# Decode attention, one core: products and folds in place, one exponential per tile with a GpSimd mask, two tiles per value accumulator

## The chip, the cores and the metric

One core of one Trainium2 chip. The metric is the device time of one execution in microseconds (us), here of the single core that runs. Engines in the profile: PE is TensorE (PEld its weight loads), DVE is VectorE, ACT is ScalarE, POOL is GpSimd, SP is SyncE, which issues nearly all loads.

## The reference

One decode step of attention plus a gated MLP, both on the same normalised input. There are 4 sequences (B), 32 heads (H), 4096 cached positions (S), head size 128 (Dh), model size 640 (D).

```python
xn = layernorm(x)                                  # x: [4, 1, 640]
q = (xn @ wq) per head                             # wq: [640, 4096]
scores = einsum('bhqd,bhkd->bhqk', q, k_cache) * Dh ** -0.5
p = softmax(scores)
o = einsum('bhqk,bhkd->bhqd', p, v_cache)          # caches: [4, 32, 4096, 128] bf16
A = o @ wo                                         # wo: [4096, 640]
z = gelu(xn @ w_in); z1, z2 = halves; z2 = layernorm(z2)
B = (z1 * (w_sp * z2 + b_sp)) @ w_out
out = x + A + B
```

The two caches are 128 MiB each and every byte of them is used once.

## The kernel before, in words

**Tiles.** The work is cut into NT = 32 tiles. A tile is HT = 4 heads of one sequence: `i = 4 * hg + b`, head group hg of 8, sequence b of 4. A K tile and a V tile are 4 MiB each: 128 partitions by NC = 128 positions by 128 values, bf16. A partition belongs to one head: each head has LN = 32 partitions ("lanes"), and each lane 128 of its 4096 positions.

**Loads.** All big loads go out on SyncE's queue, in the order of the list `loads`: k0, k1, v0, k2, v1, k3 and so on, each V one place behind the next K; with EXTRA_K two K in a row come at two places (k25 and k26, and k30 and k31 at the end). All tiles share a pool of KV_SLOTS = 5 buffers in ring order, so load n waits until the tile of load n - 5 is no longer used. `pump()` (L121 is the load in `load`) issues what the list `used` allows. `wo` is loaded by head group (`load_wo`, L155 and L153), behind the K and V loads on the same queue. The last V tile is loaded in four pieces (V_CUTS).

**Scores** (per tile, all on 128 partitions). `stage_q` spreads the query rows over the lanes with four matmuls (L383) and a copy (L391). `product` (L397, VectorE) multiplies a quarter of the K tile by the query into the tile `prod`; `fold_half` (L409, VectorE) adds the upper 64 values of each position to the lower 64 into the tile `folded`; `sums` (L421, TensorE) adds up the 64 in eight matmuls with the identity, for each half of the tile, leaving eight values a position in PSUM; `row_sums` (L432, VectorE) adds those eight.

**Softmax.** `lane_max` (L441), `turn_max` (L446, a transpose), `head_max` (L451) and `spread_max` (L462) find each head's maximum and spread its scaled negative over the lanes. `exps` copies it (L470) and runs four exponentials (L474), one per head, each on 32 partitions, writing `p_m[b]` with the other heads' places left at zero, and the sums into `acc`.

**Values.** `blocks` (L489) multiplies V by the masked exponentials, 32 matmuls that take four positions at once and use four groups of 32 output partitions; it copies the accumulator `pv_acc` (L497). `gather` (L506) picks the blocks that belong together into `pv` with `sel`. For the last pieces of the last V tile `pairs` (L518) is used. `group_den` (L530, L534) makes the denominators of a head group, `group_norm` (L539) divides and `group_proj` (L548) multiplies by `wo`.

**Order.** The main part runs under a manual schedule: on TensorE, VectorE, ScalarE and SyncE the instructions run in the order written. In iteration i the softmax of tile i - 1 is interleaved with the products of tile i, and `blocks` runs for a tile `turns[i]` that lags by 1, later by 2 and 3.

Of the kernel before, what the change touches and what calls it, by code (L numbers as in the profile page):

```python
# [20 lines left out]
def kernel(  # L21
# [31 lines left out]
    NQ = 4  # L53
    QC = NC // NQ
# [12 lines left out]
    prod = ctx.enter_context(tc.tile_pool(name="prod", bufs=1))  # L67
    fold = ctx.enter_context(tc.tile_pool(name="fold", bufs=2))
# [80 lines left out]
    def load_wo(j):  # L149
# [19 lines left out]
    scale_row = const.tile([1, P], FP32)  # L169
    nc.vector.memset(scale_row[:], scale_qk)  # L170
# [5 lines left out]
    assert GC * HT <= LN and GC * Dh * 4 <= 2048  # L176
    pv_acc = ps_acc.tile([P, GC * Dh], FP32)
    nc.vector.memset(pv_acc[:], 0.0)
    sel = const.tile([P, GC * HT], FP32)
    nc.vector.tensor_reduce(  # L180
        out=sel[:],
        in_=ident_f[:].rearrange("p (g q) -> p q g", g=CG)[:, 0 : GC * HT, :],
        axis=AX.X,
        op=ALU.add,
    )

    NACC = 2
    p_m = [const.tile([P, NC, HT], BF16, name=f"pm{b}") for b in range(Bsz)]
    acc = [const.tile([P, HT, Bsz], FP32, name=f"acc{g}") for g in range(NACC)]
    for t in p_m + acc:  # L190
        nc.gpsimd.memset(t[:], 0.0)
# [185 lines left out]
    folds, sums_ps, maxes = {}, {}, {}  # L377

    def stage_q(i):
        hg, b = divmod(i, Bsz)  # L380
        qb_ps = ps_m.tile([P, Dh], FP32, tag="m", name="qbc_ps")
        for hh in range(HT):
            nc.tensor.matmul(  # L383
                out=qb_ps[hh * LN : (hh + 1) * LN, :],
                lhsT=qT[:, HT * hg + hh, b : b + 1].to_broadcast([P, LN]),
                rhs=ident[:],
                start=True,
                stop=True,
            )
        qbcs[i] = small.tile([P, Dh], BF16, name="qbc", bufs=3)  # L390
        nc.scalar.copy(out=qbcs[i][:], in_=qb_ps[:])  # L391

    prods = {}

    def product(i, q):
        t = prods[i, q] = prod.tile([P, QC, Dh], BF16, name="prod")
        nc.vector.tensor_tensor(  # L397
            out=t[:],
            in0=k_tiles[i][:, q * QC : (q + 1) * QC, :],
            in1=qbcs[i][:, None, :].to_broadcast([P, QC, Dh]),  # L400
            op=ALU.mult,
        )

    def fold_half(i, q):
        t = prods.pop((i, q))
        half, part = divmod(q, 2)
        if part == 0:
            folds[i, half] = fold.tile([P, HC, HD2], BF16, name="folded")
        nc.vector.tensor_tensor(  # L409
            out=folds[i, half][:, part * QC : (part + 1) * QC, :],  # L410
            in0=t[:, :, 0:HD2],
            in1=t[:, :, HD2:Dh],
            op=ALU.add,
        )

    def sums(i, half):
        t = folds.pop((i, half))
        s = sums_ps[i, half] = ps_s.tile([P, HC, RW], FP32, name="s_ps")
        n = HD2 // RW
        for g in range(n):  # L420
            nc.tensor.matmul(  # L421
                out=s[:],
                lhsT=ident[:],
                rhs=t[:, :, g * RW : (g + 1) * RW],
                start=(g == 0),
                stop=(g == n - 1),
            )
# [16 lines left out]
    def turn_max(i):  # L444
        mT = ps_m.tile([1, P], FP32, tag="m", name="mT")
        nc.tensor.transpose(out=mT[:], in_=maxes[i][:], identity=ident_f[:])  # L446
        maxes[i] = mT

    def head_max(i):
        nm = small.tile([1, HT], FP32, name="nm")  # L450
        nc.vector.tensor_reduce(  # L451
            out=nm[:],
            in_=maxes[i][:].rearrange("a (h p) -> a h p", h=HT),
            axis=AX.X,
            op=ALU.max,
            negate=True,
        )
        maxes[i] = nm

    def spread_max(i):  # L460
        nb_ps = ps_m.tile([P, HT], FP32, tag="m", name="nb_ps")
        nc.tensor.matmul(  # L462
            out=nb_ps[:], lhsT=scale_row[:], rhs=maxes[i][:], start=True, stop=True
        )
        maxes[i] = nb_ps

    def exps(i):
        hg, b = divmod(i, Bsz)
        nb = small.tile([P, HT], FP32, name="nb")
        nc.scalar.copy(out=nb[:], in_=maxes.pop(i)[:])  # L470
        s_sb, pm, a = scores.pop(i), p_m[b], acc[hg % NACC]
        for hh in range(HT):
            ps = slice(hh * LN, (hh + 1) * LN)
            nc.scalar.activation(  # L474
                out=pm[ps, :, hh],
                in_=s_sb[ps, :],
                func=ACT.Exp,
                bias=nb[ps, hh : hh + 1],
                scale=scale_qk,
                accum_out=a[ps, hh, b : b + 1],  # L480
            )

    def blocks(i, c0=0, c1=NC):


        v_nat, pm = v_tiles[i], p_m[i % Bsz]
        for c in range(c0, c1, GC):
            g = c // GC % CG
            nc.tensor.matmul(  # L489
                out=pv_acc[g * LN : g * LN + GC * HT, :],  # L490
                lhsT=pm[:, c : c + GC, :].rearrange("p c h -> p (c h)"),
                rhs=v_nat[:, c : c + GC, :].rearrange("p c d -> p (c d)"),
                start=(c < GC * CG),
                stop=(c >= c1 - GC * CG),
            )
        pv_sb = work.tile([P, GC * Dh], FP32, name="pv_sb")
        nc.scalar.copy(out=pv_sb[:], in_=pv_acc[:])  # L497
        blocks_sb[i] = pv_sb

    def gather(i, stop=True):  # L500
        hg, b = divmod(i, Bsz)
        if b == 0:
            pvs[hg] = ps_pv.tile([P, HT, Bsz], FP32, tag="pv", name="pv")
        pv_sb = blocks_sb.pop(i)
        for k in range(GC):
            nc.tensor.matmul(  # L506
                out=pvs[hg][:, :, b],
                lhsT=pv_sb[:, k * Dh : (k + 1) * Dh],
                rhs=sel[:, k * HT : (k + 1) * HT],
                start=(k == 0),  # L510
                stop=stop and k == GC - 1,
            )

    def pairs(i, c0, c1):
        hg, b = divmod(i, Bsz)
        v_nat, pm = v_tiles[i], p_m[b]
        for c in range(c0, c1):
# [3 lines left out]
                rhs=pm[:, c, :],  # L521
# [6 lines left out]
    def group_den(hg):  # L528
        den = ps_m.tile([P, HT, Bsz], FP32, tag="m", name="den")
        nc.tensor.matmul(  # L530
            out=den[:], lhsT=ones_sq[:], rhs=acc[hg % NACC][:], start=True, stop=True
        )
# [40 lines left out]
    with tc.manual_schedule(engines={E.PE, E.DVE, E.Activation, E.SP}):  # L573
# [5 lines left out]
        for i in range(NT):  # L579
            j = turns.get(i)  # L580
            product(i, 0)
            fold_half(i, 0)
            at(i - 1, row_sums, 1)
            at(i - 1, lane_max)
            at(i - 1, turn_max)
            group(turns.get(i - 1, -1), group_proj)
            product(i, 1)
            at(i - 1, head_max)
            at(i - 1, spread_max)
            at(i - 1, exps)  # L590
            fold_half(i, 1)
            sums(i, 0)
            product(i, 2)
            if i + 2 < NT:
                stage_q(i + 2)
            fold_half(i, 2)
# [10 lines left out]
            product(i, 3)  # L607
            fold_half(i, 3)
# [12 lines left out]
        turn_max(NT - 1)  # L621
        head_max(NT - 1)
        spread_max(NT - 1)
# [3 lines left out]
        gather(NT - 2)  # L627
# [44 lines left out]
```

## Time and profile before

| what | value |
|---|---|
| median of 3 runs | 670.0 us (669.78 to 670.29) |
| the profiled execution's own time | 669.68 us |
| its span | 667.9 us |
| PE busy | 347.9 us (52%) |
| DVE busy | 506.7 us (76%) |
| ACT busy | 113.0 us (17%) |
| POOL busy | 2.7 us |
| read from HBM | 282.24 MB, 423 GB/s over the span |

How to read the lines: a group's line has source line, engine, operation, output from inputs, shapes, count, then total busy us and mean ns of one, then the idle us just before them and what ended it. Section 2 of the page cuts the span into 40 slices; each digit is a busy share in tenths. The chain of waits is followed back from the last instruction. Times in a timeline are us from the start of the span.

### The profile page before, as it was taken

The numbers are of one execution on the slowest core, as the hardware profiler recorded it, in microseconds if no ns is written. First come the engines' busy times: TensorE is split into PE (matmuls) and PEld (weight loads), VectorE is DVE, ScalarE is ACT, GpSimd is POOL, SyncE is SP. The second block draws the span as 40 slices with busy tenths as digits, with TensorE's granted clock in tenths as the row PEclk, the third lists the DMA queues.
The fourth block names the chain that finished last, engine by engine and source line by source line (L and its number), as shares of the span: only waits on it lengthen the run. The fifth ranks groups of instructions, "written<-read, shape, count | busy, mean of one in ns | idle before, by whom it ended". The sixth has DMA issues, their size and how long they took to land.

```text
span 667.9 us, 5968 instructions
## 1 busy us (share of the span) xinstructions
PE 347.9 (52%) x2425; PEld 154.7 (23%) x2425; DVE 506.7 (76%) x435; ACT 113.0 (17%) x361; POOL 2.7 (0%) x13
## 2 busy tenths in 40 slices
PE   1627554535557345663346654455564556546575
PEld 0502221212222122221112221122222112222133
DVE  1299897867789677787777698776787899876961
ACT  0202111101111101111101111111111111110122
POOL 1000000000000000000000000000000000000000
PEclk9997766788766678775786866788766667786677
DMA  9999999999999999999999999999999999999996
GB/s 373 418 440 433 419 433 436 420 435 426 429 426 430 433 430 429 424 431 432 434 421 432 423 434 435 428 426 429 424 435 434 421 430 432 429 422 433 432 422 257
DMA packets 14663, 282.63 MB, mean 423 GB/s; under 512 B 1344, under 2 KB 5548, under 8 KB 5932
## 3 DMA queue, kind: packets, MB, share of 16 engines
q1 hardware_dynamic: 14616, 282.25, 99.1%
q8 instruction: 19, 0.31, 0.2%
q14 instruction: 8, 0.07, 0.0%
q10 hardware_dynamic: 20, 0.01, 0.0%
HBM read 282.24 MB, written 0.01 MB: 423 GB/s over the span
## 4 chain that ended last, share of the span: by engine, by line
DMA 68%; DVE 21%; PE 8%; SPq 1%; issue 1%; DVEq 0%
DMA k_nat<-in_A_k_cache_dram 63%; DVE prod L397 13%; PE s_ps L421 7%; DVE folded L409 5%; DMA v_nat<-in_A_v_cache_dram 5%; DVE s_sb L432 2%; PE pv_acc L489 1%; SPq L121 1%; DVE m L441 1%; DVE nm L451 0%; PE out_ps L548 0%; PE qbc_ps L383 0%; SPq L90 0%; SPq L102 0%; PE den L530 0%
## 5 line engine op out<-in xcount | busy, mean ns | idle before, releaser
L397 DVE TENSOR_TENSOR prod<-k_nat,qbc 128x4096 bf16<-128x4096 bf16 x128 | 292.7, 2287 | 91.4 <-DMA k_nat<-in_A_k_cache_dram 89.9
L421 PE MATMUL s_ps<-folded,ident 128*128 128x512 bf16 x512 | 186.9, 531 | 64.7 <-DVE folded L409 64.6
L409 DVE TENSOR_TENSOR folded<-prod 128x2048 bf16<-128x2048 bf16 x128 | 156.1, 1220 | 3.3
L421 PEld LDWEIGHTS <-ident 128*128 128x128 bf16 x512 | 64.9, 128 | 152.4 <-issue 135.3
L446 PE MATMUL mT<-ident_f,m 128*1 128x128 f32 x32 | 11.0, 344 | 154.8 <-DVE m L441 154.8
L474 ACT ACTIVATE pm<-s_sb,nb 32x128 bf16<-32x128 f32 x128 | 73.9, 578 | 2.6
L470 ACT COPY nb<-nb_ps 128x4 f32<-128x4 f32 x32 | 5.2, 162 | 394.9 <-PE nb_ps L462 394.9
L489 PE MATMUL pv_acc<-v_nat,pm 128*16 128x512 bf16 x1008 | 71.7, 434 | 0.2 <-DMA v_nat<-in_A_v_cache_dram 0.2
L432 DVE TENSOR_REDUCE s_sb<-s_ps 128x64 f32<-128x512 f32 x64 | 43.5, 680 | 7.8 <-PE s_ps L421 5.4
L462 PE MATMUL nb_ps<-nm,scale_row 1*128 1x4 f32 x64 | 18.2, 353 | 56.2 <-DVE nm L451 56.2
L506 PE MATMUL pv<-sel,pv_sb 128*128 128x4 f32 x256 | 34.4, 258 | 19.5 <-ACT pv_sb L497 19.5
L446 PEld LDWEIGHTS mT<-ident_f,m 128*1 128x1 f32 x32 | 2.5, 79 | 173.1 <-DVE m L441 141.8
L506 PEld LDWEIGHTS pv<-sel,pv_sb 128*128 128x128 f32 x256 | 31.6, 195 | 32.3 <-ACT pv_sb L497 32.3
L489 PEld LDWEIGHTS <-pm 128*16 128x16 bf16 x1008 | 26.6, 102 | 32.6 <-issue 17.2
L474 ACT ACTIVATION_READ_ACCUMULATOR pm<-s_sb,nb 32x1 f32 x128 | 32.2, 251 | 0.0
L462 PEld LDWEIGHTS nb_ps<-nm,scale_row 1*128 1x128 f32 x64 | 15.5, 299 | 66.7 <-DVE nm L451 59.8
L497 ACT COPY pv_sb<-pv_acc 128x512 f32<-128x512 f32 x32 | 18.7, 585 | 61.4 <-PE pv_acc L489 61.4
L391 ACT CAST qbc<-qbc_ps 128x128 bf16<-128x128 f32 x32 | 8.4, 265 | 80.0 <-PE qbc_ps L383 80.0
L534 DVE RECIPROCAL rden<-den 128x16 f32<-128x16 f32 x8 | 2.1, 258 | 21.9 <-PE den L530 21.9
L238 DVE CAST qT<-q_ps 128x128 bf16<-128x128 f32 x1 | 0.3, 292 | 15.1 <-PE q_ps L230 15.1
L230 PE MATMUL q_ps<-xnT,wq 128*128 128x4 bf16 x160 | 4.6, 167 | 10.5 <-DMA wq<-in_A_wq_dram 10.5
L441 DVE TENSOR_REDUCE m<-s_sb 128x1 f32<-128x128 f32 x32 | 9.2, 287 | 1.1
(76 smaller groups left out, 79.2 us busy)
## 6 DMA issues: line engine op xcount, KB each, us to landing
k_nat<-in_A_k_cache_dram SPq DMA_DIRECT2D x32, 4096.0 KB, 43.3
v_nat<-in_A_v_cache_dram SPq DMA_DIRECT2D x31, 4096.0 KB, 36.6
wo<-in_A_wo_dram SPq DMA_DIRECT2D x7, 640.0 KB, 44.7
wq<-in_A_wq_dram SPq DMA_DIRECT2D x1, 4096.0 KB, 12.7
w_sb<-in_B_w_in_dram SPq DMA_DIRECT2D x1, 2160.0 KB, 19.5
v_nat<-in_A_v_cache_dram SPq DMA_DIRECT2D x1, 2048.0 KB
wq<-in_A_wq_dram SPq DMA_DIRECT2D x1, 1024.0 KB, 14.8
v_nat<-in_A_v_cache_dram SPq DMA_DIRECT2D x1, 1024.0 KB
```

What stands on the lines that cost most here:

```text
L391: nc.scalar.copy(out=qbcs[i][:], in_=qb_ps[:])
L397: nc.vector.tensor_tensor(out=t[:], in0=k_tiles[i][:, q * QC : (q + 1) * QC, :], in1=qbcs[i][:, None, :].to_broadcast([P, QC, Dh]), op=ALU ...
L409: nc.vector.tensor_tensor(out=folds[i, half][:, part * QC : (part + 1) * QC, :], in0=t[:, :, 0:HD2], in1=t[:, :, HD2:Dh], op=ALU.add,)
L421: nc.tensor.matmul(out=s[:], lhsT=ident[:], rhs=t[:, :, g * RW : (g + 1) * RW], start=(g == 0), stop=(g == n - 1),)
L432: nc.vector.tensor_reduce(out=scores[i][:, half * HC : (half + 1) * HC], in_=sums_ps.pop((i, half))[:], axis=AX.X, op=ALU.add,)
L441: nc.vector.tensor_reduce(out=m1[:], in_=scores[i][:], axis=AX.X, op=ALU.max)
L446: nc.tensor.transpose(out=mT[:], in_=maxes[i][:], identity=ident_f[:])
L462: nc.tensor.matmul(out=nb_ps[:], lhsT=scale_row[:], rhs=maxes[i][:], start=True, stop=True)
L474: nc.scalar.activation(out=pm[ps, :, hh], in_=s_sb[ps, :], func=ACT.Exp, bias=nb[ps, hh : hh + 1], scale=scale_qk, accum_out=a[ps, hh, b : ...
L489: nc.tensor.matmul(out=pv_acc[g * LN : g * LN + GC * HT, :], lhsT=pm[:, c : c + GC, :].rearrange("p c h -> p (c h)"), rhs=v_nat[:, c : c + ...
L497: nc.scalar.copy(out=pv_sb[:], in_=pv_acc[:])
L506: nc.tensor.matmul(out=pvs[hg][:, :, b], lhsT=pv_sb[:, k * Dh : (k + 1) * Dh], rhs=sel[:, k * HT : (k + 1) * HT], start=(k == 0), stop=sto ...
```

## The change

- `product` and `fold_half` work on half a K tile instead of a quarter, and write into the K tile itself; the tiles `prod` and `folded` and their pools are gone. `sums` reads its input from the K tile.
- The maximum is found without the transpose: `lay_max` (ScalarE) lays each lane's maximum on a diagonal, one matmul with `head_scale` spreads a head's 32 maxima over its lanes, and `head_max` (VectorE) reduces them on all 128 partitions.
- `exps` is one exponential on 128 partitions into a new tile `p`; a GpSimd multiplication by a head mask spreads it into `p_m[b]`.
- `blocks` of an even and the following odd tile add into one accumulator, whose 32 rows a group now hold both tiles (each tile's `p_m` is zero in the other's half). Copy and `gather` run for odd tiles alone.
- `group_den` multiplies the sums by the mask on GpSimd first.
- `stage_q` transposes the 16 query rows of a head group once in four tiles, and spreads them with one matmul per tile instead of four.
- The main loop's order follows: two products and two folds an iteration. `used`, `pump` and KV_SLOTS are as before.

```diff
-    def product(i, q):
-        t = prods[i, q] = prod.tile([P, QC, Dh], BF16, name="prod")
+    def product(i, half):
+        t = k_tiles[i][:, half * HC : (half + 1) * HC, :]
         nc.vector.tensor_tensor(
-            out=t[:],
-            in0=k_tiles[i][:, q * QC : (q + 1) * QC, :],
-            in1=qbcs[i][:, None, :].to_broadcast([P, QC, Dh]),
+            out=t,
+            in0=t,
+            in1=qbcs[i][:, None, :].to_broadcast([P, HC, Dh]),
             op=ALU.mult,
         )
...
+        t = k_tiles[i][:, half * HC : (half + 1) * HC, :]
         nc.vector.tensor_tensor(
-            out=folds[i, half][:, part * QC : (part + 1) * QC, :],
...
+            out=t[:, :, 0:HD2], in0=t[:, :, 0:HD2], in1=t[:, :, HD2:Dh], op=ALU.add
         )
...
     def sums(i, half):
-        t = folds.pop((i, half))
+        t = k_tiles[i][:, half * HC : (half + 1) * HC, :]
...
+    def lay_max(i):
+
+        d = small.tile([P, LN], FP32, name="lay")
+        nc.scalar.activation(
+            out=d[:], in_=lane_diag[:], func=ACT.Copy, scale=maxes[i][:, 0:1]
+        )
+        maxes[i] = d
+
+    def spread_max(i):
+        ps = ps_m.tile([P, LN], FP32, tag="m", name="max_ps")
+        nc.tensor.matmul(
+            out=ps[:], lhsT=head_scale[:], rhs=maxes[i][:], start=True, stop=True
+        )
+        maxes[i] = ps
...
-        for hh in range(HT):
-            ps = slice(hh * LN, (hh + 1) * LN)
-            nc.scalar.activation(
-                out=pm[ps, :, hh],
-                in_=s_sb[ps, :],
-                func=ACT.Exp,
-                bias=nb[ps, hh : hh + 1],
-                scale=scale_qk,
-                accum_out=a[ps, hh, b : b + 1],
-            )
+        nb = maxes.pop(i)
+        p = small.tile([P, NC], BF16, name="p")
+        nc.scalar.activation(
+            out=p[:],
+            in_=scores.pop(i)[:],
+            func=ACT.Exp,
+            bias=nb[:],
+            scale=scale_qk,
+            accum_out=acc[hg % NACC][:, b : b + 1],
+        )
+        e = b % 2 * GC * HT
+        nc.gpsimd.tensor_tensor(
+            out=p_m[b][:, :, e : e + GC * HT].rearrange("p g (c h) -> p g c h", h=HT),
+            in0=p[:].rearrange("p (g c) -> p g c", c=GC)[:, :, :, None].to_broadcast(
+                [P, NC // GC, GC, HT]
+            ),
+            in1=hmask_bf[:, None, None, :].to_broadcast([P, NC // GC, GC, HT]),
+            op=ALU.mult,
+        )
...
-                out=pv_acc[g * LN : g * LN + GC * HT, :],
-                lhsT=pm[:, c : c + GC, :].rearrange("p c h -> p (c h)"),
+                out=pv_acc[g * LN : (g + 1) * LN, :],
+                lhsT=pm[:, c // GC, :],
                 rhs=v_nat[:, c : c + GC, :].rearrange("p c d -> p (c d)"),
-                start=(c < GC * CG),
-                stop=(c >= c1 - GC * CG),
+                start=(i % 2 == 0 and c < GC * CG),
+                stop=(i % 2 == 1 and c >= c1 - GC * CG),
             )
+        if i % 2 == 0:
+            return
...
     def group_den(hg):
+        own = small.tile([P, HT, Bsz], FP32, name="own_sum")
+        nc.gpsimd.tensor_tensor(
+            out=own[:],
+            in0=acc[hg % NACC][:, None, :].to_broadcast([P, HT, Bsz]),
+            in1=hmask[:, :, None].to_broadcast([P, HT, Bsz]),
+            op=ALU.mult,
+        )
...
             product(i, 0)
-            fold_half(i, 0)
             at(i - 1, row_sums, 1)
             at(i - 1, lane_max)
-            at(i - 1, turn_max)
+            at(i - 1, lay_max)
+            at(i - 1, spread_max)
             group(turns.get(i - 1, -1), group_proj)
+            fold_half(i, 0)
+            at(i - 1, head_max)
+            at(i - 1, exps)
+            sums(i, 0)
             product(i, 1)
-            at(i - 1, head_max)
-            at(i - 1, spread_max)
-            at(i - 1, exps)
-            fold_half(i, 1)
-            sums(i, 0)
-            product(i, 2)
             if i + 2 < NT:
                 stage_q(i + 2)
-            fold_half(i, 2)
...
             row_sums(i, 0)
-            product(i, 3)
-            fold_half(i, 3)
+            fold_half(i, 1)
             if due:
                 gather(due[-1])
             for jj in due:
                 group(jj, group_norm)
             sums(i, 1)
             used.add(("k", i))
             pump()
```

## The prediction

> **What bounds the kernel now.** I read the page from the top: the busy shares, the forty slices, the DMA queue, then the costliest groups.
>
> ```profile
> PE 347.9 (52%) x2425; PEld 154.7 (23%) x2425; DVE 506.7 (76%) x435; ACT 113.0 (17%) x361; POOL 2.7 (0%) x13
> DMA  9999999999999999999999999999999999999996
> GB/s 373 418 440 433 419 433 436 420 435 426 429 426 430 433 430 429 424 431 432 434 421 432 423 434 435 428 426 429 424 435 434 421 430 432 429 422 433 432 422 257
> q1 hardware_dynamic: 14616, 282.25, 99.1%
> ...
> L397 DVE TENSOR_TENSOR prod<-k_nat,qbc 128x4096 bf16<-128x4096 bf16 x128 | 292.7, 2287 | 91.4 <-DMA k_nat<-in_A_k_cache_dram 89.9
> L421 PE MATMUL s_ps<-folded,ident 128*128 128x512 bf16 x512 | 186.9, 531 | 64.7 <-DVE folded L409 64.6
> L409 DVE TENSOR_TENSOR folded<-prod 128x2048 bf16<-128x2048 bf16 x128 | 156.1, 1220 | 3.3
> ```
>
> No engine is full, VectorE least far from it at 76%. The one load queue is: 282.25 MB, packets under way 99.1% of the time, a nine in every slice but the last. VectorE's largest idle time, 89.9 of 91.4 us before its products, is waiting for K to land.
>
> The chain of waits, in order of time, then gives the beat (columns: start, length, what).
>
> ```profile
> 163.09 2.30 DVE prod L397
> ...
> 177.72 0.33 SPq L121
> ...
> 223.24 2.30 DVE prod L397
> ...
> 323.43 2.29 DVE L397 TENSOR_TENSOR prod<-k_nat,qbc 128x4096 bf16<-128x4096 bf16 x1 [3.70 <-DMA k_nat<-in_A_k_cache_dram]
> ...
> 343.01 2.29 DVE L397 TENSOR_TENSOR prod<-k_nat,qbc 128x4096 bf16<-128x4096 bf16 x1 [3.71 <-DMA k_nat<-in_A_k_cache_dram]
> ```
>
> (The last two lines are from the timeline.) A tile whose product starts upon its landing follows the one before it by 343.01 - 323.43 = 19.58 us: one K and one V, 8.39 MB, at 428 GB/s, so 9.8 us a transfer. Between 163.09 and 223.24 there are three tiles in 60.15 us, 20.05 each, one `wo` load included. That is the stream's beat. VectorE's own beat shows where K lies ready: K30 starts at 614.12, K31 at 630.08, 15.96 us. VectorE has 19.58 - 15.96 = 3.6 us to spare per tile.
>
> Does the stream ever lack orders? The tile views of the two caches give the time from issue to landing:
>
> ```profile
> DMA to landing us min/median/max: 30.8/43.3/45.2
> ...
> DMA to landing us min/median/max: 29.8/36.3/45.0
> ```
>
> K first, V second. A transfer's own 9.8 us taken off, even the shortest had 29.8 - 9.8 = 20 us of other loads ahead of it. A buffer may come free up to 20 us later before a gap opens. And does the rate depend on what the engines do? Windows of 10 us (columns: PE, PEld, DVE, ACT, POOL busy, clock, DMA share, GB/s):
>
> ```profile
> 540.00:550.00 10.00, 5.92 (x27) 2.19 (x29) 9.72 (x10) 2.70 (x10) 0.00 (x0) 0.67 1.01 433
> 610.00:620.00 10.00, 4.83 (x17) 1.42 (x16) 6.90 (x7) 0.00 (x0) 0.00 (x0) 0.50 1.01 433
> 645.00:655.00 10.00, 7.68 (x91) 4.19 (x91) 2.21 (x4) 2.00 (x7) 0.00 (x0) 1.00 0.99 419
> ```
>
> 433 GB/s with VectorE full and with it idle for three tenths, 419 with it nearly idle. So faster engines do not buy bandwidth, and fewer bytes are not in the change. Last, the end, in the timeline:
>
> ```profile
> 649.38 1.89 PE L421 MATMUL s_ps<-folded,ident 128*128 128x512 bf16 x8
> 656.13 0.40 PE L530 MATMUL den<-acc,ones_sq 128*128 128x16 f32 x2 [0.81 <-ACT pm L474]
> 658.01 1.04 PE L489 MATMUL pv_acc<-v_nat,pm 128*16 128x512 bf16 x16 [0.21 <-DMA v_nat<-in_A_v_cache_dram]
> 663.04 0.59 PE L518 MATMUL pv<-pm,v_nat 128*128 128x4 bf16 x16 [0.24 <-DMA v_nat<-in_A_v_cache_dram]
> ```
>
> The last V's first half is waited for at 658.01 and its last piece at 663.04; then 4.9 us of fixed work close the span at 667.9. The profiled execution took 669.68, 1.8 us around its span, and lies 0.3 under the median of 670.0.
>
> **The change, part by part.**
>
> *Products and folds.* Rows of 4096 and 2048 results (2287 and 1220 ns) give 0.521 ns a result. A product of 8192 costs 2287 + 4096 x 0.521 = 4421 ns, a fold of 4096 costs 2287. Per tile 2 x 4.42 + 2 x 2.29 = 13.42 us against 4 x 2.287 + 4 x 1.220 = 14.03, so 0.61 saved. That the output lies on an input is priced at nothing by the rows L289 (gw onto gw, 217 ns) and L285 (another tile, 218 ns), small and f32, but the only pair there is. With two sums of 0.68, the lane maximum of 0.29 and the new head maximum (0.17 to 0.29, taken 0.2) the VectorE beat is 15.3 us against 15.96. It is hidden: VectorE starts the tile when K lands, and waits 0.6 us more.
>
> *The K buffer.* It used to be free after the fourth product, 177.72 - 163.09 = 14.6 us into the tile. Now it is held through the folds (4.42 + 0.61 + 0.29 + 2.29 + 0.2 + 4.42 + 0.68 + 2.29 = 15.2) and TensorE's second set of sums: 1.89 us at full clock, 3.58 at half, and on TensorE's queue that set stands behind the blocks (1.9 to 2.6) and, every other tile, the gather (1.05). So 17 to 22 us into the tile: 3 to 7 us later. SyncE waits in order, so the next V load and the K load and `wo` behind it go out later as well. Against the 20 us of loads already queued this costs nothing; 13 are left. The sums read eight-element runs at twice the old stride; no row shows that. From below nothing, from above twice 3.58: the product beside them (4.42) covers 0.84, the rest (2.7 for each of two sets, 5.5 a tile) would be seen by VectorE. I take nothing: the runs themselves stay the same length.
>
> *Exponentials.* Four of 578 ns with four accumulator reads of 251 and a copy of 162 become one of each and a small laying-out copy: ScalarE goes from 3.5 to about 1.1 us a tile. It was 17% busy; no wait ends on it in the beat.
>
> *The mask on GpSimd* is new: 512 results a partition from two inputs. POOL rows: a memset of 512 bf16 is 525 ns, one of 128 is 204, a select of 128 is 293. From below 0.5 us; from above, three streams instead of one, 1.6; I take 1.1. Blocks of the tile before wait for it, and with them, on TensorE's queue, the gather and the second sums. The exponential ends about 4.42 + 0.61 + 0.29 + 2.29 + 0.2 + 1.0 = 8.9 us into the tile, V of the tile before lands at 9.8, so about 1 us of the mask is covered even there. No POOL row lies beside a VectorE product: GpSimd stops at 3.3 us. What each does to the other is bounded by nothing, and by VectorE held for all 1.6 us: a beat of 15.3 to 16.9 us, under 19.58 at both ends.
>
> The Trainium skill speaks against this part. "SBUF — State Buffer", section "Who interferes with whom", says that a VectorE instruction with two SBUF inputs and a GpSimd instruction that reads SBUF shut each other out for a whole instruction. "GPSIMD Engine Reference", section 3.1, gives about 2.6 cycles an element for two inputs, by which the mask would be an estimated 1.1 us. By the two the mask may start 4.4 us late, behind a product, and VectorE's beat would be 16.4; the time would be the same 670.0, since that too is under the stream's beat.
>
> *One value accumulator for two tiles, query rows in one matmul.* Half the accumulator copies (585 ns), half the gathers (1.05 us) and three of four query matmuls go; every fourth tile a transpose and a copy (about 0.6 us) come. All on TensorE and ScalarE, beside the stream.
>
> *Start.* Some ten small VectorE operations (0.06 to 0.29 us, under 2.5 together) come before the queries, which wait for `wq` till 13.5; x was ready for it at 5.1. Hidden by 8 us.
>
> *End.* K30 starts at 614.12 as before. Two tiles of 15.3 end at 644.7, not 645.95. The last sums stood behind two copies and two gathers; one of each goes (0.59 + 1.05), so they start at about 647.5, not 649.38. Sums 1.89, row sums 0.69, maximum 0.29, laying 0.3, spread 0.4, head maximum 0.2, exponential 0.83, mask 1.1, own sums 0.3 put the denominator at 653.5, not 656.13. The saving ends there: TensorE then waits for V31 at 658.01, as now. With the mask at 1.6 and both tiles held for as much, it is 657, still in time. Blocks, copy, gather and pairs after 658.01 are the same count of instructions.
>
> Sum: nothing in the middle, nothing at the start, nothing at the end. 669.7 for an execution like the profiled one, 670.0 for the median.
>
> **The rivals.** A run of this kernel (669.78 to 670.29) can hardly tell less than 0.2%, 1.3 us, from no change.
>
> *GpSimd takes the beat* (slower). If mask and product exclude each other and the mask is long, VectorE's beat passes the stream's. It decides from 19.58 - 15.3 = 4.3 us of hold per tile; each us beyond costs about 29 us over the tiles, so 5 us gives 690. Against: it needs three times my upper bound. For: no row of the trace shows it. 7%.
>
> *Larger strides or in-place work run slower* (slower). The 5.5 us of the sums at half rate would pass the 4.3 by 1.2, about 705. Against it, the unchanged run length and the L289 pair. 5%.
>
> *The end slips.* If GpSimd's two new steps, which TensorE must await before the last V, take 4.5 us more than I allow, every us after that is paid: 671 to 673. 6%.
>
> *The late release opens gaps.* It takes 20 us, three times what I find; each release then pays the rest, 675 or so. 3%.
>
> *The stream gets denser* (faster). At the end it runs at 386 GB/s (655 to 660) and 234 (660 to 663) instead of some 431: (1 - 386/431) x 5 + (1 - 234/431) x 3 = 1.9 us. Recovered in full, 668.1. Nothing in the change aims there. 8%.
>
> **How the numbers follow.** The rest, 71%, is no change. Its own range is 669.0 to 671.0 (spread of the runs, and half a us for the stream). To hold 8 in 10 I reach down to 668.6 for part of the dense stream and up to 673.5 for the slipped end. Faster 8%, same 71%, slower 21%.
>
> **What would show it.** Right: the load queue at 99% again, product rows near 4421 ns and folds near 2287, VectorE's busy time down by about 20 us and its wait for K up by about as much, the last V still waited for near 658 and 663. Wrong: a product row well over 4421 ns, a POOL row of several us, VectorE waiting for sums rather than for K, or a slice of the DMA row below nine.

## The result

The changed kernel takes **668.45 us** (median of 12 runs, 667.62 to 668.57); the kernel before, on the same chip, took 669.78 (669.65 to 670.41). The ratio is **0.9976, 95% interval 0.9967 to 0.9985**: 1.3 us less, a gain of 0.15 to 0.33%. The forecast of no change, 670.0 with a range from 668.6, missed it by 0.15 us at the lower end. The profiled execution took 668.57 us, its span 666.7 (before 669.68 and 667.9), so the trace shows 1.2 us of the gain.

The page after. First the busy shares, the DMA row, the queues and the costliest groups:

```profile
PE 347.6 (52%) x2177; PEld 143.9 (22%) x2177; DVE 489.7 (73%) x319; ACT 52.5 (8%) x161; POOL 150.2 (23%) x51
...
DMA  9999999999999999999999999999999999999996
...
q1 hardware_dynamic: 14616, 282.25, 99.2%
q8 instruction: 17, 0.28, 0.2%
q14 instruction: 7, 0.06, 0.0%
...
L426 DVE TENSOR_TENSOR k_nat<-k_nat,qbc 128x8192 bf16<-128x8192 bf16 x64 | 282.8, 4418 | 104.7 <-DMA k_nat<-in_A_k_cache_dram 103.9
L502 POOL TENSOR_TENSOR pm<-p,hmask_bf 128x512 bf16<-128x512 bf16 x32 | 142.4, 4451 | 500.4 <-ACT p L493 500.4
...
L435 DVE TENSOR_TENSOR k_nat<-k_nat 128x4096 bf16<-128x4096 bf16 x64 | 151.8, 2372 | 0.0
...
L517 PE MATMUL pv_acc<-v_nat,pm 128*32 128x512 bf16 x1008 | 84.7, 495 | 41.2 <-POOL pm L502 37.3
```

Nearly everything that the prediction wanted to see is there. The load queue is at 99%, the DMA row has a nine in every slice but the last; a product is 4418 ns (4421 worked out); VectorE is busy 17 us less and waits 14 us more for K (103.9, was 89.9). One of the signs that it had listed for being wrong is there as well, a POOL row of several us: 4451 ns a mask, where 1.1 us was taken. The two lines `q8` and `q14` were not among those read before the change. They carry the cores' instructions over the same 16 DMA engines, and before they read:

```profile
q8 instruction: 19, 0.31, 0.2%
q14 instruction: 8, 0.07, 0.0%
```

The tile views of the caches (K first, V second), the release of the buffers:

```profile
DMA to landing us min/median/max: 30.8/39.5/42.8
...
DMA to landing us min/median/max: 28.7/34.1/41.7
```

The medians fell from 43.3 and 36.3: buffers come free later by 2 to 4 us, and the shortest V load still has 19 us of other loads ahead of it. No gap opened. The windows, with the columns of before:

```profile
540.00:550.00 10.00, 6.18 (x45) 2.23 (x44) 9.96 (x8) 1.33 (x5) 4.57 (x1) 0.79 1.02 439
610.00:620.00 10.00, 2.43 (x12) 0.86 (x10) 7.36 (x4) 0.32 (x1) 0.00 (x0) 0.50 1.00 433
645.00:655.00 10.00, 6.14 (x47) 2.59 (x46) 1.17 (x3) 0.82 (x3) 1.21 (x2) 0.75 0.97 412
```

Much the same rates. The beat, in the timeline after:

```profile
302.71 4.42 DVE L426 TENSOR_TENSOR k_nat<-k_nat,qbc 128x8192 bf16<-128x8192 bf16 x1 [5.97 <-DMA k_nat<-in_A_k_cache_dram]
...
322.15 4.42 DVE L426 TENSOR_TENSOR k_nat<-k_nat,qbc 128x8192 bf16<-128x8192 bf16 x1 [4.42 <-DMA k_nat<-in_A_k_cache_dram]
```

That is 19.44 us, against the 19.58 read before. But the tile ahead of that pair, in the timeline of before, began at

```profile
303.98 2.29 DVE L397 TENSOR_TENSOR prod<-k_nat,qbc 128x4096 bf16<-128x4096 bf16 x1 [6.43 <-DMA k_nat<-in_A_k_cache_dram]
```

and 323.43 - 303.98 = 19.45. The bare beat was nearly the same; what was read as the beat held something more: in the kernel before, two instruction fetches start in between, at 334.8 and 335.2 us. And the end, in the timeline:

```profile
645.26 1.89 PE L444 MATMUL s_ps<-k_nat,ident 128*128 128x512 bf16 x8
...
649.97 1.04 POOL L502 TENSOR_TENSOR pm<-p,hmask_bf 128x512 bf16<-128x512 bf16 x1 [9.55 <-ACT p L493]
...
654.94 0.61 PE L569 MATMUL den<-own_sum,ones_sq 128*128 128x16 f32 x2
656.31 1.90 PE L517 MATMUL pv_acc<-v_nat,pm 128*32 128x512 bf16 x16 [0.76 <-DMA v_nat<-in_A_v_cache_dram]
...
660.67 1.85 PE L550 MATMUL pv<-pm,v_nat 128*128 128x4 bf16 x64
662.56 0.17 DVE L576 TENSOR_TENSOR o_n<-pv,rden 128x16 bf16<-128x16 f32 x1 [6.71 <-PE pv L550]
```

TensorE still waits for the last V, as forecast. But that V comes at 656.31 instead of 658.01. **The stream itself ended 1.7 us sooner**, with the same bytes, the same queue and the same order. That is what had to be explained.

How the landings were read: every transfer is split over 16 DMA engines, and the trace has one completion record of each engine for each transfer (a packet of 4 bytes). Data land when the slowest of the 16 is done. At the end of V29 (a tile without pieces, near the end) the 16 completions lay:

| kernel | fastest | slowest | last `wo` landed |
|---|---|---|---|
| before | 638.14 | 642.71 | 664.30 |
| after | 637.79 | 641.22 | 662.52 |

The engines don't march together: they drift 3 to 5 us apart over the run, and the slowest decides. In all 18 traces of this study the execution's time is 6.9 to 7.8 us more than the end of the last V packet (662.55 before, 660.83 after), so this landing carries the time.

### The profile page after: what moved, and what is told of

It is laid out like the page before. It is cut to its first block, busy times and chain, and to the rows that moved or that the text cites. A ratio compares the mean times of both kernels' runs of the same rounds, so it can differ in the third digit from the quotient of the medians.

```text
span 666.7 us, 5266 instructions
## 1 busy us (share of the span) xinstructions
PE 347.6 (52%) x2177; PEld 143.9 (22%) x2177; DVE 489.7 (73%) x319; ACT 52.5 (8%) x161; POOL 150.2 (23%) x51
## 4 chain that ended last, share of the span: by engine, by line
issue 49%; DMA 25%; POOL 15%; DVE 6%; PE 4%; SPq 0%; ACT 0%; POOLq 0%; DVEq 0%; ACTq 0%
DMA k_nat<-in_A_k_cache_dram 21%; POOL pm L502 15%; DVE k_nat L426 4%; DMA v_nat<-in_A_v_cache_dram 4%; DVE k_nat L435 2%; PE s_ps L444 2%; PE pv_acc L517 1%; PE pv L538 0%; DVE s_sb L455 0%; PE pv L550 0%; PE out_ps L585 0%; ACT pv_sb L527 0%; POOL own_sum L562 0%; DVE m L464 0%; SPq L86 0%
## 5 line engine op out<-in xcount | busy, mean ns | idle before, releaser
L426 DVE TENSOR_TENSOR k_nat<-k_nat,qbc 128x8192 bf16<-128x8192 bf16 x64 | 282.8, 4418 | 104.7 <-DMA k_nat<-in_A_k_cache_dram 103.9
L502 POOL TENSOR_TENSOR pm<-p,hmask_bf 128x512 bf16<-128x512 bf16 x32 | 142.4, 4451 | 500.4 <-ACT p L493 500.4
L444 PE MATMUL s_ps<-k_nat,ident 128*128 128x512 bf16 x512 | 193.1, 545 | 63.2 <-DVE k_nat L435 63.2
L435 DVE TENSOR_TENSOR k_nat<-k_nat 128x4096 bf16<-128x4096 bf16 x64 | 151.8, 2372 | 0.0
L477 PE MATMUL max_ps<-lay,head_scale 128*128 128x32 f32 x64 | 19.0, 388 | 179.5 <-ACT lay L470 179.5
L517 PE MATMUL pv_acc<-v_nat,pm 128*32 128x512 bf16 x1008 | 84.7, 495 | 41.2 <-POOL pm L502 37.3
L477 PEld LDWEIGHTS max_ps<-lay,head_scale 128*128 128x128 f32 x64 | 14.8, 288 | 199.4 <-ACT lay L470 199.4
L517 PEld LDWEIGHTS <-pm 128*32 128x32 bf16 x1008 | 29.7, 116 | 82.8 <-POOL pm L502 43.6
L455 DVE TENSOR_REDUCE s_sb<-s_ps 128x64 f32<-128x512 f32 x64 | 43.3, 676 | 4.6 <-PE s_ps L444 4.6
L538 PE MATMUL pv<-sel,pv_sb 128*128 128x8 f32 x128 | 19.4, 278 | 9.1 <-ACT pv_sb L527 9.1
L538 PEld LDWEIGHTS pv<-sel,pv_sb 128*128 128x128 f32 x128 | 17.9, 216 | 15.8 <-ACT pv_sb L527 15.8
```

Of the source, the lines that this page charges most:

```text
L426: nc.vector.tensor_tensor(out=t, in0=t, in1=qbcs[i][:, None, :].to_broadcast([P, HC, Dh]), op=ALU.mult,)
L435: nc.vector.tensor_tensor(out=t[:, :, 0:HD2], in0=t[:, :, 0:HD2], in1=t[:, :, HD2:Dh], op=ALU.add)
L444: nc.tensor.matmul(out=s[:], lhsT=ident[:], rhs=t[:, :, g * RW : (g + 1) * RW], start=(g == 0), stop=(g == n - 1),)
L455: nc.vector.tensor_reduce(out=scores[i][:, half * HC : (half + 1) * HC], in_=sums_ps.pop((i, half))[:], axis=AX.X, op=ALU.add,)
L477: nc.tensor.matmul(out=ps[:], lhsT=head_scale[:], rhs=maxes[i][:], start=True, stop=True)
L502: nc.gpsimd.tensor_tensor(out=p_m[b][:, :, e : e + GC * HT].rearrange("p g (c h) -> p g c h", h=HT), in0=p[:].rearrange("p (g c) -> p g c" ...
```

## The experiments

Theories, with the letters that the expectations use. **A** (later **F**): the program has 702 fewer instructions, so fewer instruction fetches stand in the DMA engines' way. **B**: the engines' own traffic to the on-chip memory (in-place products, fewer tiles written) had been slowing the loads. **C**: the order at the end. **P**: the place of the K and V buffers in the on-chip memory, which moved because the sizes of other tiles changed. **S**: the added ScalarE copies disturb by themselves. Medians stand beside the kernel before on the same chip.

### e1 and e2: more instructions

```diff
+    pad_t = const.tile([1, 2], FP32, name="pad")
+    nc.vector.memset(pad_t[:], 0.0)
+    def pad(n):
+        for _ in range(n):
+            nc.scalar.copy(out=pad_t[:, 1:2], in_=pad_t[:, 0:1])
...
             pump()
+            if 1 <= i <= 28:
+                pad(25)      # e2: pad(50)
```

e1 is the changed kernel with 700 one-element copies on ScalarE, e2 the kernel before with 1400.

> The changed kernel with 700 one-element ScalarE copies added (25 at the end of each of the iterations 1 to 28, where ScalarE is idle), which brings the instruction count from 5266 back to about 5966. Theory A (the load stream got denser because 0.045 MB fewer instructions are fetched over the same 16 DMA engines): back to 669.5 to 670, the instruction queue's packets from 17 to 19 or 20, the last V tile's first half waited for at about 658 instead of 656.3. Theory B (the stream is denser because products and folds no longer write tiles of their own, that is, because of the engines' memory traffic): unchanged, 668.4. Theory C (only the order of work at the very end differs): unchanged, 668.4.

Measured 669.51 against 670.03, ratio 0.9993 (0.9984 to 1.0002): 0.5 of the 1.3 us is left, and the interval includes no gain, though VectorE, GpSimd and the wait structure are those of the changed kernel.

> The kernel before with 1400 one-element ScalarE copies added (50 at the end of each of the iterations 1 to 28). Theory A: the same dose again, twice: 1400 instructions are 0.09 MB more to fetch, 672.0 to 673, five or six more packets on the instruction queue. Theories B and C: 669.8, unless ScalarE's 10 us of copies hold up the exponentials, which the profile would show as TensorE waiting for ScalarE.

Measured 669.05, ratio 0.9988 (0.9979 to 0.9998). This missed: with twice as many copies the kernel before became *faster*. Either theory A was wrong, or something else had moved. The allocation shows what: the pad tile is 32 bytes a partition, and the pools behind it moved by 32. The K and V buffers began at 24800 bytes in the kernel before (224 modulo 256), at 30112 after (160), at 30144 in e1 (192) and at 24832 in e2 (0).

### e3 and e4: in place alone, and a control

e3 is the kernel before with products and folds by halves in the K tile, all else and the buffers' place unchanged:

```diff
-        t = prods[i, q] = prod.tile([P, QC, Dh], BF16, name="prod")
+        t = k_tiles[i][:, half * HC : (half + 1) * HC, :]
```

> The kernel before with the products and folds in place by halves alone; softmax, mask, accumulator and query rows as before. VectorE's instructions fall by 128, so the program is 2% shorter. Theory A: 669.5, a quarter or less of the gain. Theory B: all of the gain in the stream, 668.5 to 669. Theory C: 669.8.

Measured 670.45, ratio 1.0005 (0.9996 to 1.0014). The main part of the change does nothing alone; theory B, which needed it, fell.

e4 is the kernel before again, unchanged.

> The kernel before, unchanged, for a second trace of it on the same chip as the others: how much the interval between two tiles' landings and the end of the load stream differ from trace to trace with nothing changed. All theories: ratio 1.000; the last V tile's first half waited for at 657.5 to 658.5. If it is waited for near 656.5, the shift between the first two traces is no effect of the change.

Measured 669.98, ratio 1.0 (0.9992 to 1.0009); the last V was waited for at 658.21. One profile's landing is good to some 0.2 us.

### e5 to e8: the place of the buffers apart from the instructions

```diff
+    gap_t = const.tile([P, N], FP32, name="gap")   # N: e5 8, e6 24, e7 80, e8 120
+    nc.vector.memset(gap_t[:, 0:1], 0.0)
     NACC = 2
```

An unused tile moves the pools. e5 is the kernel before with its buffers at 0 modulo 256; e6 the changed kernel at 0; e7 the changed kernel at 224, where the kernel before has them; e8 is e2 put back to 224.

> The kernel before with one unused tile of 32 bytes a partition set in front of the K and V buffers (and one memset): their SBUF offset goes from 24800 (224 modulo 256) to 24832 (0 modulo 256), as it was by accident with the 1400 copies. No other edit. Theory P (the place of the buffers sets the time of a load packet): 32 KB packets at 1213 ns as there instead of 1214 to 1224, tiles 9.68 us apart a transfer instead of 9.72, 64 of them: 667 to 667.8. Theory S (the ScalarE copies themselves made the stream denser): 669.9, packets as before.

> The changed kernel with 96 unused bytes a partition in front of the buffers: offset 30112 (160 modulo 256) becomes 30208 (0). Theory P: 64 transfers of 9.68 us instead of 9.714, 2.2 us less of stream, 666.3, perhaps 666.8 if TensorE's last chain takes over the end. Theory S: 668.4.

> The changed kernel with 320 unused bytes a partition, so that its buffers stand at 224 modulo 256, as in the kernel before. If the gain of the change is the place alone: 669.8 to 670. If it is the slowest DMA engine alone (fewer instruction fetches on it, theory F): 668.4. If both: packets as in the kernel before, 9.721 us a transfer, half a us of the 1.3 lost: 668.9.

> The kernel before with the 1400 ScalarE copies and its buffers put back to 224 modulo 256. Theory F with theory P: the gain of the place is gone and the cost of the fetches stays, packets of 1214 to 1224 ns and a slowest DMA engine 2 to 3 us further behind: 671.5 to 673. Theory S: 669.0 as with the copies and the buffers at 0. Neither fetches nor copies matter, only the place: 669.9.

| run | place mod 256 | median us | ratio (95%) | 32 KB packet, mean ns | slowest engine, V29 |
|---|---|---|---|---|---|
| before | 224 | 670.21 | | 1222.0 | 642.71 |
| e5 | 0 | 665.47 | 0.9937 (0.9925 to 0.9950) | 1216.3 | 638.69 |
| e6 | 0 | **664.15** | **0.9914** (0.9900 to 0.9927) | 1216.0 | 637.72 |
| e7 | 224 | 668.87 | 0.9981 (0.9972 to 0.9990) | 1221.7 | 641.69 |
| e8 | 224 | 674.54 | 1.0068 (1.0054 to 1.0082) | 1222.3 | 647.69 |

(In this table before's median is that of its runs beside e5 to e8, its other values are from its own trace.) Theory P is shown: 32 unused bytes make the kernel before 4.7 us faster with no instruction of its loop changed, and the changed kernel gains 4.3. A row of a K or V tile, one packet of 32 KB, takes 1213 ns at 0, near always; at 224 it takes 1214 to 1224, most often 1216. Between transfers the engines then need 9.681 us instead of 9.721, and 64 transfers by 0.04 are 2.6 us. All load packets together, the small ones and the delayed ones too, took 661.8 us an engine in the kernel before and 657.8 in e5, 4.0 less. The last V is waited for 3.7 us sooner than before in e5, and 3.7 sooner than after the change in e6:

```profile
654.35 1.88 PE L492 MATMUL pv_acc<-v_nat,pm 128*16 128x512 bf16 x16 [1.20 <-DMA v_nat<-in_A_v_cache_dram]
```

```profile
652.64 1.90 PE L520 MATMUL pv_acc<-v_nat,pm 128*32 128x512 bf16 x16 [0.76 <-DMA v_nat<-in_A_v_cache_dram]
```

The profiled execution of e5 took 666.60 us, 1.1 more than the median of its runs, so the last us of the 4.7 is in no trace.

But the changed kernel's own gain is not mainly that. At before's place (e7) it still has 1.3 us: the move from 224 to 160 shortened the packet by 1 ns, 9.714 us a transfer, 0.45 us over 64. In the timeline of e7 the last V is waited for at 656.78, 0.47 later than after the change and 1.23 sooner than before:

```profile
656.78 1.90 PE L520 MATMUL pv_acc<-v_nat,pm 128*32 128x512 bf16 x16 [1.49 <-DMA v_nat<-in_A_v_cache_dram]
```

e8 then shows the other term. With the place of before, 1400 copies cost 4.3 us. Its page has 11 more fetches in `q14`:

```profile
PE 350.9 (52%) x2425; PEld 155.0 (23%) x2425; DVE 507.2 (75%) x437; ACT 379.3 (56%) x1761; POOL 2.8 (0%) x13
...
q8 instruction: 19, 0.31, 0.2%
q14 instruction: 19, 0.16, 0.1%
```

and in its timeline the last V is waited for at 662.87:

```profile
662.87 1.04 PE L499 MATMUL pv_acc<-v_nat,pm 128*16 128x512 bf16 x16 [0.38 <-DMA v_nat<-in_A_v_cache_dram]
```

The 16 completions at V29's end say how 11 fetches of 8 KB, 0.32 us each, become 4.3 us: the fastest engine is at 638.15, as before (638.14), the middle at 641.31 (641.14), and the slowest at 647.69 (642.71). Of these three only the slowest was delayed. Its completions, normally 9.72 us apart, are 10.39 to 10.45 apart ten times, at 193, 234, 283, 325, 364, 406, 445, 487, 526 and 567 us, each within 10 us behind a fetch (188, 228, 275, 317, 356, 398, 437, 480, 524, 562). The packets say where 0.68 us comes from. Each of these ten fetches is followed at its end by one 32 KB packet of 1593 to 1596 ns instead of 1216: 0.31 us for the fetch and 0.38 for the longer packet are 0.69. Theory F is shown for added instructions. It also explains e2: at a multiple of 256 the same copies cost 3.6 us (669.05 against 665.47 in e5), less than the place brings.

Could the copies have delayed the loads by holding the engines up (S)? The waits of e8 (columns: us in total, times, longest) have them in VectorE's way:

```profile
DVE prod L407 <- DMA k_nat<-in_A_k_cache_dram: 54.7, 16, 5.6
DVE prod L407 <- ACT pad L385: 38.6, 11, 5.4
```

But the sum, 93.3 us, is near the 89.9 of before: a copy ends last where otherwise the landing would have. And no load is issued late: the shortest time from issue to landing is 30.5 us for K and 30.7 for V, so that 20 us of other loads are ahead of each, as before.

### e9 to e11: the parts alone

At before's place: e9 has the query rows in one matmul, e10 the new softmax with one exponential and GpSimd's mask, e11 the in-place products and two tiles to one accumulator (the accumulator alone finds no room beside the product tiles, so it wasn't tried).

```diff
# e9
-        for hh in range(HT):
-            nc.tensor.matmul(
-                out=qb_ps[hh * LN : (hh + 1) * LN, :],
...
+        nc.tensor.matmul(
+            out=qb_ps[:], lhsT=q_lanes[:, b, :], rhs=q_rows[hg][:], start=True, stop=True
+        )
# e10: kernel before with lay_max, spread_max, head_max, exps, group_den of the change
# e11: e3 with blocks, gather, pairs and sel of the change
```

> The kernel before with the query rows in one matmul alone, buffers at 224 modulo 512 as before. About 180 TensorE instructions fewer (11 KB, under one fetch of 16 KB). Theory F (what is left of the gain, 0.9 us, comes from fewer instruction fetches on the slowest DMA engine): between 669.2 and 670.2, with the slowest engine's lag falling by one fetch (1.1 us) only if one of its fetches falls away. Theory C (the end of the kernel is shorter): 670.1, the end has no part of this edit.

> The kernel before with the new softmax alone (maximum by lay and spread, one exponential, mask and own sums on GpSimd), products by quarters, blocks and gather as before, buffers at 224 modulo 512. ScalarE has about 190 instructions fewer (12 KB, one or two of its 8 KB fetches). Theory F: 669.3 to 670.2 by which engine loses a fetch. Theory C: 669.5 or more, since the last softmax is 2.5 us shorter and the last V waits for DMA anyway. If GpSimd's masks, held up by VectorE's products, cost anything: over 671, with TensorE waiting for POOL at the end.

> The kernel before with the products and folds in place and two tiles to one accumulator (the accumulator alone doesn't fit into the memory with the product tiles), buffers at 224 modulo 512; to be held against the run with the in-place work alone, 670.45. Half the gathers and accumulator copies: 128 TensorE matmuls with their weight loads and 16 ScalarE copies fewer, 16 KB, one fetch. Theory F: 669.4 to 670.5. Theory C: 670 or less, one gather and one copy fewer stand before the last tile's sums.

Measured 669.77 (ratio 0.9999, 0.9990 to 1.0008), 669.81 (1.0, 0.9992 to 1.0009) and 669.84 (0.9999, 0.9990 to 1.0008). No part alone brings anything, GpSimd's mask costs nothing, and a fetch or two less (18 packets in `q8` in all three) are no gain as such.

### e12: fewer instructions still, at the aligned place

e6, and a second fold from 64 to 32 values, so that four matmuls instead of eight make a half's sums:

```diff
+        nc.vector.tensor_tensor(
+            out=t[:, :, 0:HD4], in0=t[:, :, 0:HD4], in1=t[:, :, HD4:HD2], op=ALU.add
+        )
...
-        n = HD2 // RW
+        n = HD4 // RW
```

> The changed kernel with its buffers at 0 modulo 512 and a second fold in place (64 values to 32), so that four matmuls instead of eight add up each half tile: 256 matmuls and 256 weight loads fewer, 32 KB, two fetches of 16 KB; VectorE has two folds of 128x2048 more a tile, 2.44 us, a beat of about 17.7 us under the stream's 19.4. Theory F: 663 to 664.2, two fetches fewer among 16 engines. If VectorE's beat comes too near the stream's, later releases of K and a later last tile: 665 or more.

Measured 664.25, ratio 0.9917 (0.9904 to 0.9931): like e6. TensorE does 50 us less and VectorE 78 us more, at 86%, and neither reaches the end; 455 instructions less bring nothing here either.

### e13 to e16: added instructions at the right place, two parts together, another place

e13 is e1 with its buffers at 224, to be compared with e7. e14 is the change without the softmax part, e15 the change without the query part, both at 224. e16 is the changed kernel at 128 modulo 256.

```diff
+    gap_t = const.tile([P, N], FP32, name="gap")   # e13 72, e16 56
# e14: e11 and e9 together;  e15: the changed kernel with stage_q of before
```

> The changed kernel with 700 one-element ScalarE copies (25 in each of the iterations 1 to 28) and its buffers at 224 modulo 512, the place of the kernel before. To be held against 668.87, the same without the copies. Theory F (fewer instruction fetches on the slowest DMA engine carry the 0.9 us): 669.8 to 670.6, the slowest engine about 1 us later at the last V tile. If the 0.9 us comes from the order of work instead: 668.9.

> In-place products and folds, two tiles per accumulator and query rows in one matmul, the softmax as before; buffers at 224 modulo 512. Theory F: 669.2 to 670, half the gain or less, since ScalarE's 190 instructions (one or two fetches of 8 KB) are back. If ScalarE's instructions don't count: 668.9.

> The changed kernel with the query rows spread by four matmuls as before; buffers at 224 modulo 512. Some 180 TensorE instructions are back, under one fetch of 16 KB. Theory F: 668.9 to 669.9, by whether the slowest engine gets that fetch. If TensorE's instructions don't count: 668.9.

> The changed kernel with its buffers at 128 modulo 256. Theory P in its strict form (a 32 KB row that starts off a 256-byte boundary needs one more transaction): packets like those at 160, 668.2 to 668.9. If a boundary of 128 bytes is enough: as with 0, 664.2. In between: the cost grows with the offset, about 666.5.

e13: 669.99, ratio 0.9998 (0.9990 to 1.0007), 1.1 us above e7, with 12 packets in `q14` instead of 7; the slowest engine at V29's end is at 643.08 (e7 641.69). The dose holds: nearly as many instructions as before (5928 to 5968), and the time of before. The order of work (theory C) is that of e7, and would have left 668.9.

e14: 669.55, ratio 0.9993 (0.9985 to 1.0002). e15: 669.95, ratio 1.0002 (0.9993 to 1.0011). Each lacks one part. e14 keeps 0.6 us of the gain and e15 0.2, and both intervals include no gain, though at V29 both have their slowest engine where e7 has it (641.61 and 641.53). What they lose, they lose behind V29. In e7 and after the change a 16 KB fetch (1.0 to 1.1 us) starts at 645 to 646, and the next at 662, when the loads are all but done; e14 has one at 660.3, and three packets of its last V trail in at 661.79, 662.13 and 662.28 when the rest had come by 661.27. In the timeline of e14:

```profile
656.71 1.05 PE L499 MATMUL pv_acc<-v_nat,pm 128*32 128x512 bf16 x16 [1.17 <-DMA v_nat<-in_A_v_cache_dram]
...
662.78 0.59 PE L532 MATMUL pv<-pm,v_nat 128*128 128x4 bf16 x16 [1.70 <-DMA v_nat<-in_A_v_cache_dram]
```

The first half lands as in e7 (656.78), the last piece 1.70 us after TensorE was ready for it. In e15 the fetch is at 648.6, as in the kernel before (649.8), and in both the last packets come in one by one, as from a single engine, about 0.16 us apart, up to 662.53 and 662.55. e11 is a third case: 641.61 at V29, then a 16 KB fetch at 645.7, and the last V waited for at 657.60. So a fetch costs by when it comes and on which engine, and the number of them only sets how often. The engine is inferred from the completions; the records don't name it.

e16: 668.03, ratio 0.9970 (0.9957 to 0.9982), packets of 1220.7 ns. A 128-byte boundary does no more than 160 or 192 do (1220.7 and 1220.8): of the places tried only multiples of 256 are fast.

## Why the prediction was wrong, and where it was right

**The step that failed** is "nothing in the middle, nothing at the start, nothing at the end", that is, the rate of the stream taken as given. It rested on windows in which engines were busy and idle, and what these show still stands (e3, e12). But "does the rate depend on what the engines do" was not the only question. Two things that no line of the diff names set it, and the change moved both:

- *Place.* Other tiles changed size, and the cache buffers went from 224 to 160 modulo 256 bytes. That is worth 0.45 us by packets and 0.47 by the landing of e7 against after. The times can't tell: the medians, 668.87 and 668.45, differ by 0.4, but so do those of the kernel before beside them (670.21 and 669.78).
- *Instruction fetches.* 5968 instructions became 5266, 27 fetches 24, and they fell later or on engines with slack. That is the rest of the 1.7 us, the 1.23 by which e7 lands before the kernel before with its buffers at the same place; 1.0 of it is there at V29 (642.71 to 641.69). In the kernel before the slowest engine's completions are 10.20 and 10.38 us apart at 603 and 613 us, behind fetches at 596 and 608; in e7 and in the changed kernel no two are more than 9.85 apart after 470 us. That fetches delay the slowest engine is shown by e8 and e13; that the missing delays make up this 1.23 is read from the completions of before, e7, e11, e14 and e15, since a fetch can't be moved alone.

The landing came 1.7 us sooner, the span shrank by 1.2. The windows of the end tell where 0.5 was given back; before first, after second:

```profile
655.00:660.00 5.00, 3.02 (x36) 1.88 (x28) 0.26 (x1) 2.23 (x6) 0.00 (x0) 1.00 0.96 386
660.00:665.00 5.00, 4.50 (x80) 3.70 (x79) 0.17 (x1) 0.00 (x0) 0.00 (x0) 0.50 0.42 153
```

```profile
655.00:660.00 5.00, 3.50 (x26) 2.10 (x24) 0.26 (x1) 0.58 (x1) 0.00 (x0) 0.50 0.96 381
660.00:665.00 5.00, 3.75 (x76) 2.78 (x76) 0.66 (x2) 0.41 (x1) 0.00 (x0) 0.50 0.25 91
```

The granted clock at 655 to 660 fell from 1.00 to 0.50, and the 16 matmuls on the last V's first half took 1.90 us instead of 1.04. Their wider output is not the reason: in e14 the same matmuls took 1.05, in e5 the narrower ones 1.88. What set the clock there no run shows. From that landing to `o_n` it was 6.25 us, before 5.65 (the line below), though the pairs no longer waited for a piece. "The same count of instructions" was right, their length was not.

```profile
663.66 0.17 DVE L539 TENSOR_TENSOR o_n<-pv,rden 128x16 bf16<-128x16 f32 x1 [6.84 <-PE pv L518]
```

**The rivals.** *The stream gets denser* (8%, 668.1) is what happened; its time was near, and half of it came the way it said, by fuller last slices. A window at a fixed time hides that (655 to 660: 386 before, 381 after), since the stream itself ends sooner. The 10 us up to the landing of the last `wo`, before first:

```profile
654.30:664.30 10.00, 7.52 (x122) 5.62 (x115) 0.43 (x2) 2.90 (x8) 0.00 (x0) 0.78 0.77 302
```

```profile
652.52:662.52 10.00, 8.51 (x114) 5.30 (x106) 0.26 (x1) 0.58 (x1) 0.00 (x0) 0.50 0.85 339
```

By the rival's own sum that is (339 - 302)/431 x 10 = 0.9 us. In the same stretch e7 has 341, and e11, e13, e14 and e15, which have little or none of the gain, 310, 290, 300 and 292. "Nothing in the change aims there" is true of the lines of the diff; the place and the fetches are not in its lines. *GpSimd takes the beat* did not happen (e10 1.0). *Larger strides or in-place work* did not: products 4418, and e3 at 1.0005. *The end slips* did not: the mask alone took 1.04 us (1.1 taken) and the denominator was there at 654.94, 1.4 later than worked out because TensorE had first to wait for V30 at 651.41, and still ahead of the last V. *Gaps* did not open.

**Right terms.** (The terms for the exponential's end add up to 8.8 us, not 8.9; nothing hangs on it.) Folds: 2287 worked out, 2.28 measured, 2.52 where they lie beside the mask, mean 2372. VectorE's beat, K30 to K31 where K lies ready, was 627.55 - 612.60 = 14.95 us, 15.3 worked out; in the timeline:

```profile
612.60 4.42 DVE L426 TENSOR_TENSOR k_nat<-k_nat,qbc 128x8192 bf16<-128x8192 bf16 x1 [4.41 <-DMA k_nat<-in_A_k_cache_dram]
...
627.55 4.41 DVE L426 TENSOR_TENSOR k_nat<-k_nat,qbc 128x8192 bf16<-128x8192 bf16 x1
```

The bound on mask and product holding each other up was needed, and it is GpSimd that pays. In the same timeline:

```profile
289.28 4.41 DVE L426 TENSOR_TENSOR k_nat<-k_nat,qbc 128x8192 bf16<-128x8192 bf16 x1
290.03 4.56 POOL L502 TENSOR_TENSOR pm<-p,hmask_bf 128x512 bf16<-128x512 bf16 x1 [14.92 <-ACT p L493]
294.21 2.52 DVE L435 TENSOR_TENSOR k_nat<-k_nat 128x4096 bf16<-128x4096 bf16 x1
```

A mask of 1.04 us is drawn out to 4.56, to 0.90 us past the product's end at 293.69, and the fold beside its end takes 2.52 us instead of 2.28. TensorE's `blocks` do wait for the masks, 37.3 us in all, but VectorE's beat stays under the stream's, so this wait doesn't reach the end. The Trainium skill's "SBUF — State Buffer", section "Who interferes with whom", says that a VectorE instruction with two inputs in SBUF contends with a GpSimd instruction that reads SBUF, and the trace agrees.

Two of its pages bear on the terms that were missing. "DMA: Bandwidth & Descriptors", section "How a descriptor splits into AXI transactions", says that a transaction starts on a 256-byte boundary, so that a descriptor that doesn't start on one pays beats for bytes it doesn't use. An estimate by it: at 224 modulo 256 a 32 KB row costs 1031 beats instead of 1024, 0.7%. It speaks of reads, and here it is the on-chip side of a load, which is written; the runs show 1222.0 against 1216.3 ns, 0.5%, and the step at 256. "Runtime: NRT & Kernel Launch", section "Instruction fetch mechanics", calls the cost of a fetch mostly hidden. No run here tells whether it is hidden from the engine that executes; for a kernel bound by its loads e8 measures 4.3 us for 11 of them.

## What to carry to other kernels

Where a load stream bounds the kernel, look at where its buffers begin in the on-chip memory before anything else: a few unused bytes that put them on a 256-byte boundary were worth 4.3 to 4.7 us here, more than three times the whole change; together with the change they make the best version of this study (e6, 664.15 us, 0.9914 with 0.9900 to 0.9927). A change that moves no byte and no order still moves addresses and instruction count; before a difference under 1% is put down to what the diff says, put the buffers back to their old place and compare again. When a rate is called fixed, ask by what: the queue's own packets, other queues on the same DMA engines, the slowest engine.

## What the runs showed of the hardware that was not expected

- A 32 KB packet into the on-chip memory took a mean of 1216.0 to 1216.3 ns where the buffers began on a multiple of 256 bytes, and of 1220.7 to 1222.3 at 128, 160, 192 and 224; 0.6 to 0.7% of this kernel's time hangs on it.
- The 16 DMA engines of a stream drift apart, 4.6 us in the kernel before and 9.5 in e8 at V29's end, and the slowest sets every landing.
- Instruction fetches go over the same engines: 16 KB at about 1.07 us and 8 KB at 0.32 with the buffers at 224 (0.95 and 0.31 in e5, at 0). At 224, behind nearly every fetch between 100 and 650 us, one load packet took 1.57 to 1.88 us instead of 1.22, so a fetch costs its engine more than its own time. ScalarE's added instructions in e8 delayed the slowest engine, ten times by 0.68 us, and neither the fastest nor the middle one.
